# Attention and expert layer on one core: batch 1's queries projected ahead of the first denominators, the first quotient in two halves, and two edits of the queues

## The chip, the core and the metric

The kernel runs on one core of a Trainium2 chip. The core has five engines that work side by side, each through its own instructions in order: TensorE (matrix products, PE in the profile, with its weight loads as PEld), VectorE (DVE), ScalarE (ACT), GpSimd (POOL) and SyncE (SP, which here only starts transfers). Sixteen DMA engines move data between the main memory, the on-chip memory and back. TensorE writes into PSUM, a small memory of eight banks; VectorE and ScalarE read it from there. The metric is the time on the device in microseconds (us), the median of several runs.

## The reference

Four batches, four heads, 1088 tokens, head size 32; the second part has 4352 = 4 x 1088 tokens of 128 numbers, 8 experts, and a hidden size of 1024. All is in single precision.

```
phi(x) = (S1 x) outer (S2 x), 8 x 8 = 64 features          # S1, S2: 8 x 32
kv = sum over tokens of phi(k) v ; z = sum of phi(k)
x  = phi(q) kv / (phi(q) z + 1e-6), heads side by side      # 4352 x 128
P  = exp(x w_gate - max), then 8 times: rows to sum 1, columns to sum N/E
out = sum over experts e of P[:, e] * (relu(x w1[e]) w2[e])
```

## The kernel before

**Expert layer.** Most of the work is `x w1[e]`, relu, `w2[e]`. The 4352 tokens are cut into groups; `items` are pairs of a group and an expert, and `blocks` cut each item by the hidden size. A group is of two token tiles (functions `two`, and `eight` or `seven`, which saves products by a Strassen-like scheme) or of three (`four`, `twenty`, with more sums and fewer products). `step(c)` of a block is one product with `w1` (`first`, L914) and a relu on ScalarE into `hb` or `hx` (L918); the second products (`into`, L1099) follow eight steps later and add up in four PSUM banks. VectorE makes sums and differences of hidden tiles (`less`, `do`). GpSimd makes sums and differences of `w2`: `sums_of_two` and `sums_of_four`. The latter (tile `ws`, 1 MB) are made once per expert (L242), stored to memory (L246), and loaded again for each later group (L230). GpSimd also multiplies a group's tokens by the routing weights (`prepare_x`, `weigh`, tile `xe`, L678), which SyncE loads by `pT` (`weights_of`, L674). Some (group, expert) pairs are worked off before the routing weights are known; their results are `kept` unweighted, weighted later by `weigh_kept` and added.

**Attention.** Batch 0 takes a way of its own so that the first tokens are ready early. Its queries are cut into three chunks: columns 0 to 511, 512 to 799, 800 to 1087. For a chunk c, `query_products(c)` (L376) makes both factors of the features, `multiply(c, i)` (L384, VectorE) multiplies them, `fractions(c, 1)` and `fractions(c, 0)` (L392) make denominators and numerators, and `divide(c)` (L403 to L410) makes the quotient on VectorE: the denominators are turned by blocks of 32, one column in 32 is kept, made reciprocal, spread and turned back, and multiplied into `xT`. `keys_kept(0)` (L362, ScalarE) copies the sums of batch 0's keys, `kvz`, which `fractions` need. Batches 1 to 3 go through `queries_ab(b)` (L426 and the copy L429 into `qab`), which projects the queries, transfers that repeat the factors (`qa`, `qb`, `repeat_a`, `repeat_b`), and `attention(b)`. `transpose_q(b)` (L297, VectorE) turns a batch's queries.

**Order.** Where `tc.manual_schedule` names engines, their instructions go in the order of the program; elsewhere a planner orders them, and `tc.keep_in_program_order` fixes single ones. The first stretch names VectorE, TensorE and ScalarE, the second VectorE and TensorE. `fill(n)` puts as many expert steps into the attention's order as pay for n: after the first quotient `fill(1.25)` gives two steps of the first block, then come `fractions(1, 1)` and `fractions(1, 0)`, then two more steps. The first group is columns 0 to 511 in two tiles of 256. Its four steps go through token tile t fastest:

```
f, t = 2 * q + c // 2, c % 2
first(k, f, t * n, (t + 1) * n, h[c], k % 2)
```

The four PSUM banks called `a` go round: every `bank()` takes the next.

Of the kernel before, what the change touches and what calls it, by code (L numbers as in the profile page):

```python
# [10 lines left out]
F32 = mybir.dt.float32  # L11
U32 = mybir.dt.uint32
Act = mybir.ActivationFunctionType
Alu = mybir.AluOpType
# [36 lines left out]
def kernel(  # L51
# [12 lines left out]
    nc = tc.nc  # L64
    P = nc.NUM_PARTITIONS
# [146 lines left out]
    stored, stored_four = {}, {}  # L212
# [13 lines left out]
    def sums_of_four(e, w2):  # L226

        ws = pools[0].tile([P, len(FORMS), FO // 4, H2], F32, tag="ws4", name="ws4")
        if e in stored_four:
            nc.sync.dma_start(out=ws, in_=stored_four[e])  # L230
            return ws

        def blocks(bs):
            b = w2[:, bs[0][1]::4, H2 * bs[0][0]:H2 * (bs[0][0] + 1)].unsqueeze(1)
            if len(bs) == 1:
                return b
            step = (bs[1][1] - bs[0][1]) * DM + (bs[1][0] - bs[0][0]) * H2
            return AP(tensor=b.tensor, offset=b.offset, ap=[b.ap[0], [step, 2], *b.ap[2:]])

        c = 0  # L240
        for ns, x, y, off in FOURS:
            tc.keep_in_program_order(nc.gpsimd.tensor_tensor(ws[:, c:c + len(ns)], blocks(x), blocks(y),  # L242
                                                             op=Alu.subtract if off else Alu.add))
            c += len(ns)
        stored_four[e] = dram.tile([P, len(FORMS), FO // 4, H2], F32, name=f"ws4{e}")
        nc.sync.dma_start(out=stored_four[e], in_=ws)  # L246
        return ws


# [45 lines left out]
    def transpose_q(b, lo=0, hi=S):  # L295
        to = kT if b == 1 else qT
        nc.vector.transpose(out=to[:, lo:hi], in_=loaded["q", b].rearrange("p a d -> p (a d)")[:, lo:hi])  # L297
# [94 lines left out]
            nc.tensor.matmul(t[64 * i:64 * (i + 1), 0:n], kvz[:, m, i].rearrange("p h d -> p (h d)"),  # L392
                             phs[0][:, i, lo:hi], start=True, stop=True, tile_position=(0, 64 * i))

    def divide(c):


        lo, hi = chunks[c]
        n = hi - lo
        nb = n // 32  # L400
        pn, pd = (queries.pop((0, c, "pn", m)) for m in range(2))
        rd = wk.tile([P, 512], F32, tag="rd", name="rd")
        nc.vector.transpose(out=rd[:, 0:n], in_=pd[:, 0:n])  # L403
        rc = wk.tile([P, 16], F32, tag="rc", name="rc")[:, 0:nb]
        nc.vector.tensor_scalar_add(rc, rd[:, 0:n].rearrange("p (b r) -> p b r", r=32)[:, :, 0], 1e-6)
        nc.vector.reciprocal(rc, rc)
        rd = wk.tile([P, 512], F32, tag="rd", name="rd")
        nc.vector.transpose(out=rd[:, 0:n].rearrange("p (b r) -> p b r", r=32),
                            in_=rc.unsqueeze(2).to_broadcast([P, nb, 32]))
        nc.vector.tensor_tensor(xT[:, lo:hi], pn[:, 0:n], rd[:, 0:n], op=Alu.mult)  # L410

# [494 lines left out]
    def first(k, f, lo, hi, out, flip):  # L908

        j = blocks[k][0]  # L910
        ph = bank()[:, 0:hi - lo]
        for s in (1, 0) if flip else (0, 1):
            sl = slice(H2 * s, H2 * (s + 1))
            nc.tensor.matmul(ph[sl], loaded_w[j][0][:, P * f + H2 * s:P * f + H2 * (s + 1)],  # L914
                             sources[j][:, lo:hi], start=True, stop=True, tile_position=(0, H2 * s))
        if len(out.shape) == 3:
            ph = ph.rearrange("p (t n) -> p t n", t=2)
        nc.scalar.activation(out=out, in_=ph, func=Act.Relu)  # L918

    def two(k):  # L920

        j, q = blocks[k]
        n = groups[items[j][0]][1]
        h, ts, (later_h, earlier_h, t13) = hs[k] = room_of(k)

        def step(c):
            f, t = 2 * q + c // 2, c % 2
            first(k, f, t * n, (t + 1) * n, h[c], k % 2)

        def less(out, a, b):  # L930
            nc.vector.tensor_tensor(out, a, b, op=Alu.subtract)  # L931

        def sums(c):
            if direct_of(j):
                return

            if k == len(blocks) - 1:
                if c == 4:
                    less(ts[0], h[1], h[0])
                    less(ts[2], h[3], ts[0])  # L940
                    less(ts[1], h[3], h[1])
                    less(ts[3], h[2], ts[2])
            elif c == 4:
                less(t13, later_h, earlier_h)
            elif c == 5:
                less(ts[2], h[3], ts[0])
                less(ts[3], h[2], ts[2])

        return 4, step, sums
# [159 lines left out]
    def steps():  # L1109

        todo, sums_at, t = {}, {}, 0
        for k in range(len(blocks) + 5):
            if k == len(blocks) - 2:
                ctx.enter_context(tc.manual_schedule(engines={engines.DVE, engines.PE, engines.Activation}))
            if k == len(blocks):
                for i, ps in enumerate(last_products()):
                    todo.setdefault(t + i, []).extend(ps)
            if k < len(blocks):
                j, q = blocks[k]
                g, e = items[j]  # L1120
                lo, n, tiles, es, weighted = groups[g]
                if q == 0:
                    for i in (j, j + 1, j + 2 if 0 < j and j + 2 < first_weighted else j):
                        if i < len(items) and i not in sources and (pools or i < first_weighted):
                            prepare_x(i)
                        if i < len(items) and i not in loaded_w and (pools or i < first_weighted):
                            prepare_w(i)
                if j == 0 and q == 2:
                    prepare_w(2)
                if q == 1 and j + 1 < first_weighted and not direct_of(j + 1) and loaded_w[j + 1][2] is None:  # L1130
                    w1, w2, _ = loaded_w[j + 1]
                    w = w1, w2, sums_of_two(items[j + 1][1], w2)
                    loaded_w.update({i: w for i in loaded_w if items[i][1] == items[j + 1][1]})
                if q == 0:
                    if weighted and 1 <= es.index(e) <= es[0] + 1:
                        weigh_kept(g, es.index(e) - 1)
                if k == len(blocks) - HELD:
                    kept_to_sums(g)
                m, step, sums_ = (four if tiles == 3 else two)(k)
                products = twenty if tiles == 3 else eight if g in DIRECT else seven  # L1140
            for c in range(m if k < len(blocks) else 4):
                if k < len(blocks):
                    step(c)
                for do in sums_at.pop(t, ()):
                    do()
                while soon:
                    soon.pop(0)()
                for b, p in todo.pop(t, ()):
                    second(b, p)
                if k < len(blocks) and c == 0:  # L1150
                    for i in range(2, 10):
                        sums_at.setdefault(t + i, []).append(lambda i=i, f=sums_: f(i))
                    if k < len(blocks) - 2:
                        for i, ps in enumerate(products(k)):
                            todo.setdefault(t + LAG + i, []).extend((k, p) for p in ps)
                share = n / 480 * (16 / 15 if g in DIRECT else 1)
                if k >= len(blocks):
                    while later:
                        later.pop(0)()
                elif later and (tiles == 3 or c % 2 or share > 0.9):  # L1160
                    later.pop(0)()
                yield share
                t += 1
        while soon:
            soon.pop(0)()
        while later:
            later.pop(0)()
# [11 lines left out]
    with tc.manual_schedule(engines={engines.DVE, engines.PE, engines.Activation}):  # L1179
        st = projections()  # L1180
        repeated(st)
        halves = ((0, NT // 2), (NT // 2, NT))
        transpose_k(0, halves)
        keys_ab(0, halves)
        transpose_q(0, *chunks[0])
        query_products(0)
        for part_ in range(3):
            keys_products(0, part_)
        keys_sums(0)
        for i in range(2):  # L1190
            multiply(0, i)
        keys_kept(0)
        transpose_q(1)
        transpose_q(0, chunks[0][1])
        fractions(0, 1)
        queries_ab(1)
        fractions(0, 0)
        query_products(1)
        repeat_a(1)
        repeat_b(1)  # L1200
        divide(0)
        load_q(2)
    with tc.manual_schedule(engines={engines.DVE, engines.PE}):
        for i in range(2):
# [66 lines left out]
```

## Time and profile before

| | before |
|---|---|
| time, median of 3 | 920.12 us (920.08 to 920.75) |
| span of the profile | 918.0 us |
| PE busy | 911.2 us (99%) |
| DVE busy | 678.9 us (74%) |
| ACT busy | 421.6 us (46%) |
| POOL busy | 204.0 us (22%) |
| DMA, mean | 140 GB/s |

The span runs from the first to the last instruction of the profiled execution; busy times are those of each engine within it. In the lines, `L392` is the line of the kernel, `a<-ph,kvz` says which tile is written from which, and `<-` in the waits says what the engine waited for. A matrix product in single precision leaves two records for each half of the array, so four for one `first`. Matrix products overlap one another, and the ends of their records are modelled.

### The profile page before, as it was taken

What the parts mean: (1) busy time and instruction counts of PE and PEld (TensorE: products, weight loads), DVE (VectorE), ACT (ScalarE), POOL (GpSimd) and SP (SyncE); (2) the same over time, 40 slices, a digit from 0 to 9 for tenths busy, and PEclk for the clock granted to TensorE, in tenths of its full rate; (3) what the DMA queues carried; (4) which work ended last, traced back from release to release, by engine and by line L of the source; (5) the groups of instructions that cost most, each with busy time, mean ns of one, the idle gap of its engine ahead of it and who ended that gap; (6) DMA issues with size and microseconds to landing.
All of it is one profiled execution on the core that took longest, in us unless ns stands there. A gap on an engine that the chain in (4) does not pass through costs nothing.

```text
span 918.0 us, 18893 instructions
## 1 busy us (share of the span) xinstructions
PE 911.2 (99%) x7442; PEld 637.4 (69%) x7442; DVE 678.9 (74%) x1173; ACT 421.6 (46%) x915; POOL 204.0 (22%) x212
## 2 busy tenths in 40 slices
PE   9999999999999999999999999999999999999997
PEld 6777544466666677777777777777777655556886
DVE  7678699888776798666975656956567976758665
ACT  3455555554444454444544444544445444445443
POOL 3121100175545421201210010110100243210220
PEclk9999999999999999999999999999999999999999
DMA  9994100213454535534364343454445456453640
GB/s 254 308 273 163 54 1 1 70 64 127 148 150 139 186 119 174 165 110 150 114 185 134 117 143 112 132 187 127 133 122 165 130 170 195 162 166 92 177 153 13
DMA packets 91305, 128.15 MB, mean 140 GB/s; under 512 B 25392, under 2 KB 69504, under 8 KB 86480
## 3 DMA queue, kind: packets, MB, share of 16 engines
q1 hardware_dynamic: 88384, 121.42, 42.7%
q0 software_dynamic: 1600, 5.36, 2.1%
q8 instruction: 58, 0.95, 0.4%
q10 hardware_dynamic: 1232, 0.16, 0.1%
q14 instruction: 31, 0.25, 0.1%
HBM read 107.88 MB, written 19.05 MB: 138 GB/s over the span
## 4 chain that ended last, share of the span: by engine, by line
PE 97%; DVE 2%; ACT 1%; issue 0%; POOL 0%; DVEq 0%; POOLq 0%
PE a L914 51%; PE s L1099 41%; PE a L347 1%; PE a L462 1%; PE a L114 1%; DVE hb L931 1%; PE a L314 0%; PE s L376 0%; PE a L426 0%; PE s L392 0%; DVE cs L602 0%; PE a L496 0%; PE a L392 0%; ACT hb L918 0%; DVE rs L596 0%
## 5 line engine op out<-in xcount | busy, mean ns | idle before, releaser
L914 PE MATMUL a<-xe,w 128*64 128x256 f32 (+1 forms) x2560 | 569.8, 470 | 0.0
L918 ACT ACTIVATE hb<-a 128x256 f32<-128x256 f32 (+4 forms) x408 | 195.0, 480 | 241.5 <-PE a L914 209.3
L914 PEld LDWEIGHTS a<-xe,w 128*64 128x64 f32 x2560 | 263.0, 137 | 50.8 <-issue 1.8
L918 ACT ACTIVATE hx<-a 128x256 f32<-128x256 f32 (+1 forms) x360 | 167.3, 465 | 213.5 <-PE a L914 191.6
L1099 PE MATMUL s<-hb,ws 128*64 128x256 f32 (+3 forms) x1312 | 256.1, 395 | 0.2 <-DVE hb L931 0.2
L1099 PE MATMUL s<-hx,ws 128*64 128x256 f32 x1280 | 233.9, 379 | 0.0
L978 DVE TENSOR_TENSOR hb<-hb 128x512 f32<-128x512 f32 (+1 forms) x204 | 133.5, 664 | 102.8 <-ACT hb L918 98.8
L978 DVE TENSOR_TENSOR hx<-hx 128x512 f32<-128x512 f32 (+1 forms) x204 | 149.8, 744 | 65.0 <-ACT hx L918 60.2
L1099 PEld LDWEIGHTS s<-hb,ws 128*64 128x64 f32 x1312 | 134.9, 137 | 87.8 <-issue 64.5
L678 POOL TENSOR_TENSOR xe<-xT,xe 128x768 f32<-128x768 f32 (+2 forms) x41 | 80.3, 1958 | 481.2 <-DMA xe<-pT 377.0
L1099 PEld LDWEIGHTS s<-hx,ws 128*64 128x64 f32 x1280 | 132.7, 137 | 71.6 <-issue 50.3
L914 PE MATMUL a<-xT,w 128*64 128x416 f32 (+3 forms) x512 | 119.7, 462 | 0.0
L1099 PE MATMUL s<-hb,w 128*64 128x256 f32 (+3 forms) x536 | 114.2, 408 | 0.0
L1099 PE MATMUL s<-hx,w 128*64 128x256 f32 x384 | 76.0, 379 | 0.0
L931 DVE TENSOR_TENSOR hb<-hb 128x416 f32<-128x416 f32 (+7 forms) x84 | 60.7, 723 | 18.0 <-ACT hb L918 14.0
L1099 PEld LDWEIGHTS s<-hb,w 128*64 128x64 f32 x536 | 54.1, 137 | 19.0 <-issue 6.5
L914 PEld LDWEIGHTS a<-xT,w 128*64 128x64 f32 x512 | 48.9, 137 | 25.5 <-issue 15.7
L242 POOL TENSOR_TENSOR ws<-w 128x256 f32<-128x256 f32 (+1 forms) x70 | 60.5, 899 | 8.1 <-DMA w<-in_moe_w_dram 5.2
L931 DVE TENSOR_TENSOR hx<-hx 128x256 f32<-128x256 f32 (+1 forms) x65 | 39.5, 612 | 24.0 <-ACT hx L918 22.8
L1099 PEld LDWEIGHTS s<-hx,w 128*64 128x64 f32 x384 | 40.8, 137 | 6.6
L978 DVE TENSOR_TENSOR pqg<-hb 128x512 f32<-128x512 f32 x68 | 40.5, 637 | 0.0
L978 DVE TENSOR_TENSOR pqg<-hx 128x512 f32<-128x512 f32 x68 | 35.0, 554 | 0.0
(181 smaller groups left out, 485.0 us busy)
## 6 DMA issues: line engine op xcount, KB each, us to landing
w<-in_moe_w_dram SPq DMA_DIRECT2D x82, 512.0 KB, 5.5
ws<-ws SPq DMA_DIRECT2D x34, 1024.0 KB, 5.0
xe<-pT SPq DMA_DIRECT2D x34, 384.0 KB, 4.1
ws<-ws SPq DMA_DIRECT2D x12, 512.0 KB, 3.6
ph<-qa SPq DMA_DIRECT2D x12, 288.0 KB, 4.7
rb<-qb SPq DMA_DIRECT2D x3, 1152.0 KB, 7.2
pb<-pT SPq DMA_DIRECT2D x6, 384.0 KB, 8.3
kx<-in_k_dram SPq DMA_DIRECT2D x4, 544.0 KB, 4.0
```

Of the source, the lines that this page charges most:

```text
L114: nc.tensor.matmul(warm[:, 0:P], ones, ones, start=True, stop=True)
L242: tc.keep_in_program_order(nc.gpsimd.tensor_tensor(ws[:, c:c + len(ns)], blocks(x), blocks(y), op=Alu.subtract if off else Alu.add))
L347: nc.tensor.matmul(pv[64 * s:64 * (s + 1), i], kp[0:n, H * t + h].rearrange("p i j -> p (i j)"), vx[0:n, slots[h], t, :], start=(t == 0 an ...
L462: nc.tensor.matmul(pn[64 * s:64 * (s + 1), t, 2 * i:2 * i + 2].rearrange("p h d -> p (h d)"), ph[:, i, s, 64 * t:64 * (t + 1)], kvs[b % 2] ...
L678: tc.keep_in_program_order(nc.gpsimd.tensor_tensor(out, x, pb, op=Alu.mult))
L914: nc.tensor.matmul(ph[sl], loaded_w[j][0][:, P * f + H2 * s:P * f + H2 * (s + 1)], sources[j][:, lo:hi], start=True, stop=True, tile_posit ...
L918: nc.scalar.activation(out=out, in_=ph, func=Act.Relu)
L931: nc.vector.tensor_tensor(out, a, b, op=Alu.subtract)
L978: nc.vector.tensor_tensor(out if not isinstance(out, tuple) else places(*out), places(*a), places(*b) if isinstance(b, tuple) else b, op=A ...
L1099: nc.tensor.matmul(sums[g][i][H2 * s:H2 * (s + 1), n * place:n * (place + 1)], w, x, start=c == 1, stop=c == per, tile_position=(0, H2 * s))
```

## The change

It has four parts. First, the queries of batch 1 are turned (`transpose_q(1)`) ahead of the products of chunk 0, and projected (`queries_ab(1)`) ahead of the first denominators, so that TensorE has work while ScalarE copies `kvz`. Second, `divide` can work in parts, and the first quotient is done in two halves of 256 columns; the first block's steps go through the hidden tile fastest, so that the first two need the first half alone. Third, the sums of `sums_of_four` are stored by GpSimd's queue instead of SyncE's, so that SyncE's later loads don't stand behind a store that waits for GpSimd. Fourth, `weigh_kept` comes in the second block of an item instead of the first.

```diff
         stored_four[e] = dram.tile([P, len(FORMS), FO // 4, H2], F32, name=f"ws4{e}")
-        nc.sync.dma_start(out=stored_four[e], in_=ws)
+        tc.keep_in_program_order(nc.gpsimd.dma_start(out=stored_four[e], in_=ws))
         return ws
...
-    def divide(c):
+    def divide(c, parts=1):
         lo, hi = chunks[c]
-        n = hi - lo
+        n = (hi - lo) // parts
         nb = n // 32
         pn, pd = (queries.pop((0, c, "pn", m)) for m in range(2))
...
+        for i in range(0, hi - lo, n):
+            rd = wk.tile([P, 512], F32, tag="rd", name="rd")
+            nc.vector.transpose(out=rd[:, 0:n], in_=pd[:, i:i + n])
+            rc = wk.tile([P, 16], F32, tag="rc", name="rc")[:, 0:nb]
+            nc.vector.tensor_scalar_add(rc, rd[:, 0:n].rearrange("p (b r) -> p b r", r=32)[:, :, 0], 1e-6)
+            nc.vector.reciprocal(rc, rc)
+            rd = wk.tile([P, 512], F32, tag="rd", name="rd")
+            nc.vector.transpose(out=rd[:, 0:n].rearrange("p (b r) -> p b r", r=32),
+                                in_=rc.unsqueeze(2).to_broadcast([P, nb, 32]))
+            nc.vector.tensor_tensor(xT[:, lo + i:lo + i + n], pn[:, i:i + n], rd[:, 0:n], op=Alu.mult)
...
         def step(c):
-            f, t = 2 * q + c // 2, c % 2
-            first(k, f, t * n, (t + 1) * n, h[c], k % 2)
+            f, t = (c % 2, c // 2) if k == 0 else (c // 2, c % 2)
+            first(k, 2 * q + f, t * n, (t + 1) * n, h[2 * f + t], k % 2)
...
-                if q == 0:
-                    if weighted and 1 <= es.index(e) <= es[0] + 1:
-                        weigh_kept(g, es.index(e) - 1)
+                if q == 1 and weighted and 1 <= es.index(e) <= es[0] + 1:
+                    weigh_kept(g, es.index(e) - 1)
...
         keys_sums(0)
+        transpose_q(1)
         for i in range(2):
             multiply(0, i)
         keys_kept(0)
-        transpose_q(1)
         transpose_q(0, chunks[0][1])
+        queries_ab(1)
         fractions(0, 1)
-        queries_ab(1)
         fractions(0, 0)
         query_products(1)
         repeat_a(1)
         repeat_b(1)
-        divide(0)
+        divide(0, 2)
         load_q(2)
```

More of the change, by code (lines that the diff above doesn't have):

```diff
@@ L393, in fractions @@
                              phs[0][:, i, lo:hi], start=True, stop=True, tile_position=(0, 64 * i))
-    def divide(c):
+    def divide(c, parts=1):
         lo, hi = chunks[c]
-        n = hi - lo
+        n = (hi - lo) // parts
         nb = n // 32
         pn, pd = (queries.pop((0, c, "pn", m)) for m in range(2))
[L402 to L410, printed above, removed]
+        for i in range(0, hi - lo, n):
[8 more added lines that the diff above has]
+            nc.vector.tensor_tensor(xT[:, lo + i:lo + i + n], pn[:, i:i + n], rd[:, 0:n], op=Alu.mult)
     def queries_ab(b):
```

## The prediction

> **What bounds the kernel now.** I read first the page's slices and the chain of work that ended last, which say that TensorE is never out of work for long:
>
> ```profile
> PE   9999999999999999999999999999999999999997
> PEclk9999999999999999999999999999999999999999
> ...
> PE 97%; DVE 2%; ACT 1%; issue 0%; POOL 0%; DVEq 0%; POOLq 0%
> ```
>
> Then the busy time by stretches, to see where the remaining 3% lie. The columns are length, then busy time of PE, PEld, DVE, ACT and POOL:
>
> ```profile
> 12.60:13.40 0.80, 0.17 (x7) 0.03 (x4) 0.80 (x2) 0.52 (x2) 0.00 (x0) 1.00 1.21 304
> 13.40:18.45 5.05, 5.05 (x36) 2.51 (x36) 4.11 (x10) 1.74 (x5) 2.25 (x4) 1.00 1.12 278
> 18.45:100.00 81.55, 81.55 (x1076) 61.71 (x1076) 63.31 (x111) 38.74 (x102) 15.79 (x27) 1.00 0.76 229
> 200.00:912.00 712.00, 712.00 (x5548) 514.73 (x5545) 513.82 (x880) 318.04 (x678) 166.80 (x133) 1.00 0.45 141
> ```
>
> From 13.4 us on TensorE has no hole: 81.55 of 81.55 us, and 712.00 of 712.00. A busy PE need not be PE at its peak, so I also read the starts of single matmuls. A pair on the two halves of the array starts every 0.216 us at 256 columns, 0.430 at 512, and outside the changes of shape (0.05 to 0.16 us each) I find no late start between 200 us and the end. The only place with free time is the stretch from 12.6 to 13.4 us. The waits of TensorE in the whole run name it:
>
> ```profile
> PE a L114 <- POOL own L116: 1.0, 1, 1.0
> PE a L392 <- ACT kvz L362: 0.6, 1, 0.6
> PE s L1099 <- DVE hb L931: 0.2, 1, 0.2
> ```
>
> The chain of waits from 12 us shows what follows it, and VectorE's timeline shows how close that engine runs beside it (start, duration):
>
> ```profile
> 13.39 1.08 PE a L392 x4
> 14.47 0.98 PE a L426 x12
> 15.45 0.86 PE a L392 x4
> 16.31 1.17 PE s L376 x8
> 17.48 1.01 PE a L914 x8
> 18.49 1.15 PE s L392 x8
> ```
>
> ```profile
> 14.55 0.72 DVE L403 STREAM_TRANSPOSE rd<-a 128x512 f32<-128x512 f32 x1 [0.46 <-PE a L392]
> 15.30 0.17 DVE L405 TENSOR_SCALAR rc<-rd 128x16 f32<-128x16 f32 x1
> 15.51 0.25 DVE L406 RECIPROCAL rc<-rc 128x16 f32<-128x16 f32 x1
> 15.79 0.71 DVE L408 STREAM_TRANSPOSE rd<-rc 128x512 f32<-128x512 f32 x1
> 16.61 0.69 DVE L410 TENSOR_TENSOR xT<-a,rd 128x512 f32<-128x512 f32 x1
> 17.58 0.82 DVE L384 TENSOR_TENSOR ph<-ph,s 128x288 f32<-128x288 f32 x2 [0.28 <-PE s L376]
> ```
>
> The reader is to see that the quotient (14.55 to 17.30) and the second chunk's products (17.58 to 18.40) end just as TensorE wants them: L914 starts at 17.41, L392 at 18.45. Two engines run level here, so work added to VectorE is not hidden.
>
> [...] a transposition takes 0.72 us at 512 columns and 0.44 at 288, the mean of L384's products falls only from 0.67 to 0.45. [...] Here the seven stores of ws4 take 0.33 us each on SyncE's queue, and what they cost there is the wait ahead of them (111.4 us in 7, longest 17.0, for GpSimd's sums). [...] the hole of 0.8 us did not lower the clock (1.00), and I take the same for a wait of 1.6.
>
> **The change, part by part.**
>
> *Batch 1's queries earlier.* On VectorE the turn of the queries (L297, 12.14 to 13.36 by start of the next) goes ahead of the two products L384 (10.94 to 12.14). Their sum is the same: turn 10.94 to 12.16, products to 13.36. The queries' load has landed by 10.67 by its semaphore, so 0.27 us are left. On TensorE the last L347 leaves the array free at 12.60. The projections (L426, 0.98) now stand next; their kT is there at 12.2, so they fill the hole: 12.70 (0.10 for the change of shape, as L347 to L914 at 30.5) to 13.68. The denominators L392 then start at 13.68 instead of 13.39; kvz is there at 13.35, the products at 13.4. The numerators follow at 14.59 (0.91 as before), L376 at 15.55 (0.96), and TensorE is free for L914 at 16.72 (1.17) instead of 17.41. So TensorE has 0.69 us in hand, but the denominators are 0.29 us later. The copy qab and the DMAs behind it (qa, qb) start about 1.6 us earlier; nothing on TensorE waits for them, and the wait for rb that follows (4.6 us on VectorE at 32.8) holds no matmul.
>
> *First quotient in two halves, first steps reordered.* Before, VectorE's first read came 1.16 us after the denominators' start (14.55 less 13.39): now 13.68 + 1.16 = 14.84. The whole chain took 17.30 - 14.55 = 2.75. For 256 columns I take the rows at 512 and 288: transposition 0.72 - 256 x (0.28/224) = 0.40, twice; product 0.69 - 256 x (0.23/224) = 0.43; the two small operations and the gaps as before. That is 2.75 - 0.32 - 0.31 - 0.26 = 1.86, checked by the 288-column chain at 19.60 to 21.58 (1.98). The first half is ready at 16.70. L914 starts 0.10 after it (as before: 17.30 to 17.41), 16.80, with TensorE free since 16.72. Its two steps need only columns 0 to 255, since the new order takes both F tiles on token tile 0 first. They end at 17.75.
>
> Next on TensorE are the fractions of chunk 1 (L392), which wait for the products L384 of chunk 1. These stand in VectorE's order behind the second half, which is the wait that the change adds: second half 16.64 to 18.50 (an independent operation starts 0.06 before the last ends), products 18.44 to 19.26, L392 at 19.31. Before, it was 18.45. Behind the waiting L392 stand all later matmuls; TensorE sits idle from 17.75 to 19.31, 1.56 us, where it lost 0.13 before. Net: 19.31 - 18.45 = 0.86 us later. The extra VectorE work is 2 x 1.86 - 2.75 = 0.97; the chain also starts 0.29 later and loses the 0.28 us wait that stood before L384. 0.97 + 0.29 - 0.28, less 0.06 at each of two joints, is again 0.86.
>
> The bounds: with a transposition of 0.38 or 0.48 and a product of 0.40 or 0.46, a half is 1.79 to 2.05, so the delay is 0.7 to 1.2 us. Afterwards TensorE is at work without a hole to 912 us, so no later slack can take the delay back; transposition of the keys (L302) and the second quotient move with it, and L314 finds its kT at 20.6, before TensorE comes (21.2).
>
> *Stores by GpSimd's queue.* It removes SyncE's seven waits. It adds seven issues on GpSimd; the trace has the like of them (xd, L486: 0.59 us; xt's 576 KB), so 0.6 x 7 = 4 us beside 204 us busy of 918. Behind each stand the kept sums and the next weighted tokens xe. The tightest case before: xe was ready at 240.17 (238.17 + 2.00), and TensorE's first weight load with it was at 241.05. It was that late since its load stood behind the store (227.76) and the kept product before it waited 8.53 us for pb. Both loads may now go earlier by up to 14 us, so 0.6 us more on GpSimd doesn't show. Worth: 0, since TensorE waited for neither.
>
> *Kept sums one block later.* The order on GpSimd stays xe, sums, kept. At the end the sums are done at 877.7 and TensorE loads them at 882.4. A block there is 3.88 us, so at worst 0.8 us are left. Worth: 0.
>
> Sum: +0.86 us, so 920.12 + 0.86 = 921.0.
>
> **Rivals.** (a) Faster: if the second half hid behind TensorE's work, as the change means it to, L392 would start at 17.85 (17.75 + 0.10) and the end come 0.60 earlier: 919.5. For it speaks that TensorE is free 0.69 us earlier; against it VectorE's order, in which nothing stands between half two and the products. At most the hole and the late start go, 0.80 + 0.13: 919.2. (b) Slower by more: the queries land 0.5 us or more later (DMA is at 1.10 of its share there, and only 0.27 us are in hand), and turn, products and denominators move: up to 0.8 us more, 921.8. (c) A new hole later: a store on GpSimd holds up xe or ws4; if the 0.6 us of each of seven came through, 4 us more, 925. Against it stands the freed SyncE queue. (d) The delay is lost in the changes of shape near 22 to 23 us (0.16 and 0.21 us): 920.6, which is no change.
>
> **How the numbers follow.** Forecast 0.60, (a) 0.15, (b) 0.10, (c) 0.05, (d) 0.10. The bound of 0.2% is 1.84 us. The forecast, (a) and (d) lie within it. Faster by 1.84 us would need more than the 0.93 us of free time that the trace has: 0.03. Slower by 1.84 needs (c), or (b) with the upper bound of the halves (1.2 + 0.8 = 2.0): 0.08. Same 0.89. The range goes from 919.2 (a) to 922.1 (b with the upper bound).
>
> **What would show it.** Right: TensorE waits at L392 for DVE ph L384 for about 1.5 us from 17.8 to 19.3; no wait for ACT kvz; L426 starts near 12.7; L914 near 16.8; the quotient's rows come twice, 256 columns each, about 0.40 us a transposition; 200 to 912 without a hole. Wrong: L392 of chunk 1 before 18.4, a wait of the turn for DMA qx, or a wait of TensorE for GpSimd past 180 us.

## The result, and the profile after

| | before | after |
|---|---|---|
| time, median of 6 | 920.13 us (919.5 to 920.75) | 923.0 us (922.62 to 923.8) |
| ratio, 95% interval | | 1.0031 [1.0018, 1.0044] |
| span of the profile | 918.0 us | 921.1 us |

The change made the kernel 0.3% slower, and the time lies above the range that was forecast (919.2 to 922.1). First the waits of TensorE after the change (total, times, longest):

```profile
PE s L1101 <- DVE hx L980: 2.5, 2, 2.3
PE a L114 <- POOL own L116: 1.0, 1, 1.0
PE s L392 <- DVE ph L384: 0.7, 1, 0.7
PE a L314 <- DVE kT L302: 0.4, 1, 0.4
PE s L1101 <- DVE hb L933: 0.2, 1, 0.2
```

The wait for `kvz` is gone, the wait of L392 for the products is there and is smaller than forecast, and the first line is new. TensorE's timeline shows where that one stands (start, duration, and in brackets how long TensorE was idle ahead and for what):

```profile
198.69 0.59 PE L915 MATMUL a<-xe,w 128*64 128x256 f32 x2
201.56 0.65 PE L1101 MATMUL s<-hx,ws 128*64 128x256 f32 x4 [2.28 <-DVE hx L980]
...
205.48 0.65 PE L1101 MATMUL s<-hx,ws 128*64 128x256 f32 x4 [0.23 <-DVE hx L980]
```

From the starts of single matmuls, TensorE has nothing to do for about 2.4 us before 201.56 and for about 0.4 before 205.48. Up to there the chain of waits runs 0.30 us late (L314 at 20.81 instead of 20.51, L915 at 189.81 instead of 189.52). 0.3 + 2.4 + 0.4 = 3.1 us, the whole difference of the spans (921.1 - 918.0). So at most a tenth of the loss is in the part that I had worked out, and nine tenths are in a place where I saw none.

The chain that ended last names VectorE for it, one operation of 7.73 us. The two timelines of VectorE at that point, before and then after:

```profile
192.62 0.56 DVE L741 TENSOR_TENSOR z<-x,z 128x384 f32<-128x384 f32 x1 [1.77 <-ACT x L750]
193.12 0.69 DVE L978 TENSOR_TENSOR hx<-hx 128x512 f32<-128x512 f32 x1
```

```profile
192.91 7.73 DVE L742 TENSOR_TENSOR z<-x,z 128x384 f32<-128x384 f32 x1 [1.91 <-ACT x L751]
200.57 0.94 DVE L980 TENSOR_TENSOR hx<-hx 128x512 f32<-128x512 f32 x1
```

The same sum of 384 columns takes 0.56 us before and 7.73 after. It is not a sum for TensorE at all (it gathers a group's unweighted results), but the sum of `hx` that TensorE needs stands behind it and starts at 200.57 instead of about 193.1. What GpSimd does meanwhile, before and then after:

```profile
182.97 8.62 POOL L242 TENSOR_TENSOR ws<-w 128x256 f32<-128x256 f32 x10
197.62 1.92 POOL L678 TENSOR_TENSOR xe<-xT,xe 128x768 f32<-128x768 f32 x1 [6.03 <-DMA xe<-pT]
199.50 8.85 POOL L242 TENSOR_TENSOR ws<-w 128x256 f32<-128x256 f32 x10
```

```profile
192.45 0.60 POOL L246 DMA_DIRECT2D ws<-ws  x1 [0.30 <-POOL ws L242]
193.07 1.83 POOL L679 TENSOR_TENSOR xe<-xT,xe 128x768 f32<-128x768 f32 x1
194.85 6.10 POOL L242 TENSOR_TENSOR ws<-w 128x256 f32<-128x256 f32 x10
201.25 0.61 POOL L246 DMA_DIRECT2D ws<-ws  x1 [0.30 <-POOL ws L242]
```

Before, GpSimd rests for 6.03 us ahead of `xe`, because SyncE issued the load of `xe` behind the store. SyncE's issues, before and then after:

```profile
191.61 0.32 SPq L246 DMA_DIRECT2D ws<-ws  x1
191.98 0.43 SPq L674 DMA_DIRECT2D xe<-pT  x1
```

```profile
175.63 0.81 SPq L675 DMA_DIRECT2D xe<-pT  x2
```

After, that load is the second of these two and went out at 176.0, 16 us earlier, so GpSimd issues the store and runs straight on for 7.9 us (193.07 to 200.95). VectorE's sum begins during the issue and ends only 0.3 us before that run does. Both engines read from the main on-chip memory, SBUF; the sum of `z` reads both of its operands there.

### The profile page after: what moved, and what is told of

Read it like the earlier page. It is cut to its first block, busy times and chain, and to the rows that moved or that the text cites. A ratio compares the mean times of both kernels' runs of the same rounds, so it can differ in the third digit from the quotient of the medians.

```text
span 921.1 us, 18903 instructions
## 1 busy us (share of the span) xinstructions
PE 911.3 (99%) x7442; PEld 533.7 (58%) x7442; DVE 682.1 (74%) x1178; ACT 421.9 (46%) x915; POOL 207.6 (23%) x219
## 3 DMA queue, kind: packets, MB, share of 16 engines
q0 software_dynamic: 2608, 12.70, 3.8%
## 4 chain that ended last, share of the span: by engine, by line
PE 94%; DVE 4%; ACT 1%; DMA 1%; issue 0%; SPq 0%; DVEq 0%; ACTq 0%
PE a L915 49%; PE s L1101 42%; PE a L347 1%; DVE z L742 1%; PE a L463 1%; DVE hb L933 1%; DMA kx<-in_k_dram 1%; PE a L314 0%; PE a L427 0%; DVE hx L980 0%; PE s L376 0%; PE s L392 0%; DVE cs L603 0%; PE a L497 0%; DVE w L742 0%
## 5 line engine op out<-in xcount | busy, mean ns | idle before, releaser
L915 PE MATMUL a<-xe,w 128*64 128x256 f32 (+1 forms) x2560 | 516.2, 470 | 0.0
L915 PEld LDWEIGHTS a<-xe,w 128*64 128x64 f32 x2560 | 200.1, 137 | 86.6 <-issue 1.6
L1101 PE MATMUL s<-hb,ws 128*64 128x256 f32 (+3 forms) x1312 | 228.7, 395 | 0.2 <-DVE hb L933 0.2
L1101 PE MATMUL s<-hx,ws 128*64 128x256 f32 x1280 | 205.4, 379 | 2.5 <-DVE hx L980 2.5
L1101 PEld LDWEIGHTS s<-hb,ws 128*64 128x64 f32 x1312 | 104.9, 137 | 116.8 <-issue 86.9
L1101 PEld LDWEIGHTS s<-hx,ws 128*64 128x64 f32 x1280 | 102.4, 137 | 103.5 <-issue 74.2
L915 PE MATMUL a<-xT,w 128*64 128x416 f32 (+3 forms) x512 | 119.7, 462 | 0.0
L1101 PE MATMUL s<-hb,w 128*64 128x256 f32 (+3 forms) x536 | 106.9, 408 | 0.0
L1101 PE MATMUL s<-hx,w 128*64 128x256 f32 x384 | 67.8, 379 | 0.0
L915 PEld LDWEIGHTS a<-xT,w 128*64 128x64 f32 x512 | 49.0, 137 | 25.5 <-issue 15.7
L1101 PEld LDWEIGHTS s<-hb,w 128*64 128x64 f32 x536 | 46.8, 137 | 24.0 <-issue 6.5
L1101 PEld LDWEIGHTS s<-hx,w 128*64 128x64 f32 x384 | 33.2, 137 | 11.5
```

The costliest lines, as they stand in the source:

```text
L1101: nc.tensor.matmul(sums[g][i][H2 * s:H2 * (s + 1), n * place:n * (place + 1)], w, x, start=c == 1, stop=c == per, tile_position=(0, H2 * s))
```

## The experiments

Two questions stood at first: which part of the change makes the loss, and, if it is the stores, what about them: the transfer issued by GpSimd itself, the run without a pause that the earlier load allows, or the two together.

**Which part of the change.** Four kernels: three with some parts alone, one with the stores left out. Parts 1 and 2 were not tried apart.

```diff
# stores alone, on the kernel before
-        nc.sync.dma_start(out=stored_four[e], in_=ws)
+        tc.keep_in_program_order(nc.gpsimd.dma_start(out=stored_four[e], in_=ws))
```

> Kernel before with the stores of ws4 on GpSimd's queue alone; the order on TensorE, VectorE and ScalarE stays that of before. Theory 1 (the stores' queue makes the late hole: the next weighted tokens come earlier, GpSimd works without a pause from about 183 to 201 us, and a VectorE operation with two on-chip inputs starves beside it): z<-x,z near 192.6 takes several us instead of 0.56, TensorE waits about 2 to 3 us near 201 us, time +2 to +3 us, 922 to 923. Theory 2 (the front's shift of 0.3 us is needed for the collision, or the kept sums are): z<-x,z stays below 2.2 us, no wait of TensorE near 201, time within 0.5 of before.

```diff
# parts 1 and 2 alone: the changed kernel with these undone
-        tc.keep_in_program_order(nc.gpsimd.dma_start(out=stored_four[e], in_=ws))
+        nc.sync.dma_start(out=stored_four[e], in_=ws)
-                if q == 1 and weighted and 1 <= es.index(e) <= es[0] + 1:
-                    weigh_kept(g, es.index(e) - 1)
+                if q == 0:
+                    if weighted and 1 <= es.index(e) <= es[0] + 1:
+                        weigh_kept(g, es.index(e) - 1)
```

> Kernel before with the first two parts alone: queries of batch 1 earlier, first quotient in halves with the reordered steps; stores and kept sums as before. Theory 1: the front costs 0.3 us (L392 of chunk 1 at 18.75 instead of 18.45) and nothing comes back later, no hole near 201: 920.4. Theory 2 (the front's shift alone makes the late collision): a hole of 2 to 3 us near 201, 923.

Part 4 alone is the last edit of that diff, turned round, on the kernel before:

> Kernel before with the kept sums one block later, nothing else. Theory 1: no part in it, no hole of TensorE beyond those of before, within 0.3 us of before. Theory 2 (the kept sums' place makes GpSimd's pile): a hole above 1 us.

The changed kernel with the first edit of that diff only, so all but the stores:

> The changed kernel with the stores of ws4 back on SyncE's queue. Theory 1: the hole near 201 us goes, z<-x,z takes about 0.6 us, the front's 0.3 stays: 920.4, 2.6 below the changed kernel. Theory 2: the hole stays, 923.

| kernel | time | ratio to before | sum of `z` |
|---|---|---|---|
| stores alone | 923.78 us | 1.0038 [1.0025, 1.0050] | 7.70 us |
| parts 1 and 2 alone | 919.96 | 0.9994 [0.9985, 1.0002] | 0.56 |
| kept sums later alone | 920.16 | 1.0003 [0.9994, 1.0011] | 0.56 |
| all but the stores | 919.83 | 0.9997 [0.9989, 1.0006] | 0.56 |

The stores alone make the whole loss; the other parts, alone or together, can't be told from no change. The 0.3 us that was expected of the front in two of them (920.4) doesn't show in the times, and the stores alone came out a little above the expected 922 to 923. The trace of the stores alone has the same picture, VectorE and GpSimd:

```profile
193.70 7.70 DVE L741 TENSOR_TENSOR z<-x,z 128x384 f32<-128x384 f32 x1 [1.93 <-ACT x L750]
```

```profile
193.21 0.60 POOL L246 DMA_DIRECT2D ws<-ws  x1 [0.30 <-POOL ws L242]
193.82 1.82 POOL L678 TENSOR_TENSOR xe<-xT,xe 128x768 f32<-128x768 f32 x1
195.60 6.10 POOL L242 TENSOR_TENSOR ws<-w 128x256 f32<-128x256 f32 x10
```

TensorE's new holes in it are 2.36 us at 202.31 and six of 0.19 to 0.42 in the 4.4 us behind it, 4.04 together. The other 1.1 us of its longer span (923.1 less 918.0) come from a wait at 35.12, long before the first of these stores. The profile puts it down to ScalarE's `hb`, but that was done at 34.19. The matmul (L462) also reads `ph`, and VectorE's product for it (L453) starts at 34.06 instead of 32.79, since the transfer `rb` lands later in this execution. Neither the kernel before nor the change has this wait in its trace, and three of the kernels below have one of 0.2 to 0.6 us there, with and without a loss in their times, so I count it as no part of the stores' cost.

**The earlier load without the transfer by GpSimd.** The stores stay on SyncE's queue, but behind the next load of `xe`, on the kernel before. GpSimd then runs without a pause, and issues nothing.

```diff
-        nc.sync.dma_start(out=stored_four[e], in_=ws)
+        pending.append((stored_four[e], ws))
...
         xe = weights_of(e, lo, t * n, "xe")
+        while pending:
+            to, ws = pending.pop()
+            tc.keep_in_program_order(nc.sync.dma_start(out=to, in_=ws))
```

> Kernel before, stores of ws4 still on SyncE's queue but each issued behind the next weighted tokens' load, so that GpSimd's run of xe and sums follows the first sums without a pause and without a transfer issued by GpSimd. Theory P (a run of GpSimd's operations without a pause is enough to starve a VectorE operation with two on-chip inputs): z<-x,z near 192.6 takes 6 to 8 us and TensorE waits 2 to 3 us near 201, 922.5 to 923. Theory D (the VectorE operation must begin while GpSimd issues a transfer): z takes at most 2.3 us, as long as the xe beside it, no wait above 0.5 us near 201, within 0.5 of before.

Measured: 919.72 us, ratio 0.9994 [0.9985, 1.0002]. GpSimd, then VectorE:

```profile
187.71 4.53 POOL L242 TENSOR_TENSOR ws<-w 128x256 f32<-128x256 f32 x6
192.20 1.82 POOL L678 TENSOR_TENSOR xe<-xT,xe 128x768 f32<-128x768 f32 x1
193.98 10.92 POOL L242 TENSOR_TENSOR ws<-w 128x256 f32<-128x256 f32 x10
```

```profile
193.27 1.17 DVE L744 TENSOR_TENSOR z<-x,z 128x384 f32<-128x384 f32 x1 [1.76 <-ACT x L753]
194.36 1.21 DVE L981 TENSOR_TENSOR hx<-hx 128x512 f32<-128x512 f32 x1
```

The run without a pause is there, but the sum of `z` waits only for the end of `xe` (193.27 + 1.17 = 194.44, `xe` ends at 194.02), and then the two engines take turns: ten sums of GpSimd need 10.92 us instead of 6.10, and VectorE's operations about 1.2 instead of 0.7. No hole of TensorE follows. The run alone is not the cause.

**The transfer by GpSimd without the earlier load.** The store on GpSimd's queue, and on SyncE's queue a copy of one small block of `ws` (32 KB) in its old place, so that `xe` comes as late as before.

```diff
-        nc.sync.dma_start(out=stored_four[e], in_=ws)
+        tc.keep_in_program_order(nc.gpsimd.dma_start(out=stored_four[e], in_=ws))
+        gate = dram.tile([P, H2], F32, name=f"gate{e}")
+        nc.sync.dma_start(out=gate, in_=ws[:, len(FORMS) - 1, FO // 4 - 1])
```

> Kernel before with the stores of ws4 on GpSimd's queue, and on SyncE's queue a small copy of the last sums (32 KB) that waits for GpSimd as the store did, so that the next weighted tokens come as late as before. Theories P and D both: GpSimd pauses after the store, z<-x,z stays below 1.3 us, no wait near 201, within 0.5 us of before. Theory Q (the transfer itself, in GpSimd's queue, does the harm): z long and a hole of 2 to 3 us as in the changed kernel.

Measured: 920.15 us, ratio 1.0001 [0.9992, 1.0009]. GpSimd, then VectorE:

```profile
192.79 0.60 POOL L246 DMA_DIRECT2D ws<-ws  x1 [0.30 <-POOL ws L242]
197.60 2.12 POOL L680 TENSOR_TENSOR xe<-xT,xe 128x768 f32<-128x768 f32 x1 [4.21 <-DMA xe<-pT]
```

```profile
193.53 0.56 DVE L743 TENSOR_TENSOR z<-x,z 128x384 f32<-128x384 f32 x1 [1.76 <-ACT x L752]
```

The same transfer, issued by the same engine at the same place, cost nothing here, where GpSimd rests 4.21 us behind it. Neither half makes the loss; both together do.

**Is it the operand?** The kernel with the stores alone, where the sum of `z` reads its first operand from PSUM:

```diff
-            add_now(z, p, z)
+            add_now(z, s if g == PLAIN - 1 else p, z)
```

> Stores on GpSimd's queue as in the store-only kernel, and the one VectorE sum z<-x,z of the last unweighted group reads its first input from PSUM instead of the copy of it. Theory of the shared input (P or D): this sum takes about 0.5 us beside GpSimd's run; the next operation with two on-chip inputs may be caught in its place. If it is not, no hole; if it is, it stands out with 5 to 7 us. Theory O (VectorE is held as a whole, whatever it reads): z itself takes about 7.7 us again.

Measured: 922.03 us, ratio 1.0019 [1.0012, 1.0026]. VectorE:

```profile
193.96 0.56 DVE L741 TENSOR_TENSOR z<-s,z 128x384 f32<-128x384 f32 x1 [1.91 <-ACT x L750]
194.46 7.36 DVE L978 TENSOR_TENSOR hx<-hx 128x512 f32<-128x512 f32 x1
201.74 0.94 DVE L978 TENSOR_TENSOR pqg<-hx 128x512 f32<-128x512 f32 x1
```

The sum of `z` begins during GpSimd's issue (193.49 to 194.09) as it did with the stores alone, and takes 0.56 us; the next operation, with both operands in SBUF, is caught in its place. It began at 194.46, when the issue was over and `xe` was running. So the operation with both operands in SBUF was held (7.36 us), the one with an operand in PSUM was not (0.56), and the held one needn't have begun during the issue. Half of the loss stays.

**Alone, first try.** A small kernel that computes none of the reference: VectorE adds 384 columns again and again beside runs of ten GpSimd sums of 256 columns, without a transfer, with one issued by GpSimd ahead of the run, and with that and one operand in PSUM.

> Not the reference's computation at all: VectorE alone with sums of 384 columns, 24 in a row, beside GpSimd with ten sums of 256 columns in a row, six times each in three stretches: without a transfer, with a 1 MB store issued by GpSimd ahead of the ten, and with that store while VectorE's first input lies in PSUM. Undisturbed a sum takes about 0.56 us. Theory P: single sums of 6 to 7 us in the first two stretches. Theory D: 1 to 1.5 us at most in the first, 6 to 8 us in the second only. Both: no sum above 0.7 us in the third.

It didn't show the effect. With two operands in SBUF the engines took turns in both phases, one for one (ten sums of GpSimd 9.71 us behind a transfer); no VectorE operation was above 1.35 us, and the means were alike (738 ns with the transfer, 726 without); with one in PSUM it was 557 ns. But all the sums of GpSimd wrote the same tile, so each waited for the one before on GpSimd's own semaphore (13.0 us of idle time ahead of 180 sums), which the kernel's sums don't. The next experiment takes these waits out.

**Alone, without those pauses.** Each sum has a tile of its own. The transfer is also smaller here, 32 KB instead of 1 MB, and waits for a result of GpSimd as the kernel's store does. One execution, with each phase three times.

```diff
-                for i in range(10):
-                    tc.keep_in_program_order(nc.gpsimd.tensor_tensor(y[:, 0:256], w[:, 1024:1280], w[:, 1280:1536], op=Alu.add))
+                y = big.tile([P, 10, 256], F32, name=f"y{name}{r}")
+                for i in range(10):
+                    if name == "pause" and i == 4:
+                        sums(y[:, i], y[:, i - 1], e)
+                    else:
+                        sums(y[:, i], b, e)
```

> Not the reference's computation: VectorE adds two 384-column operands in SBUF (in the last phase one of them in PSUM) beside runs of ten GpSimd sums of 256 columns that each have a tile of their own, so that no sum waits for another. Theory: it is the issue of a transfer by GpSimd, with no pause behind it, [...]. Then without it (plain) VectorE's operations take about 0.96 us each beside the sums, as in the phases with pauses; behind GpSimd's transfer (gdma) the first one takes 6 to 8 us; with one sum made to wait for the one before it (pause) it takes about 3 to 4 us, to the fifth sum; with the transfer issued by SyncE (sdma) 0.96 us again; from PSUM 0.56 us. Rival: the small experiment lacks something else that the kernel has (broadcast operands, what the other engines do), and no phase shows an operation above 2.5 us.

One pass of each phase from GpSimd's timeline, without the last phase; `yplain` has no transfer, `ysdma` one by SyncE, `ygdma` one by GpSimd, `ypause` too, with a fifth sum that reads the fourth's result:

```profile
24.84 10.02 POOL L41 TENSOR_TENSOR yplain<-w 128x256 f32<-128x256 f32 x10
...
80.51 0.56 POOL L57 DMA_DIRECT2D storegdma<-xgdma  x1 [0.30 <-POOL xgdma L41]
81.09 6.83 POOL L41 TENSOR_TENSOR ygdma<-w 128x256 f32<-128x256 f32 x10
...
143.44 2.75 POOL L41 TENSOR_TENSOR ypause<-w 128x256 f32<-128x256 f32 x4
146.27 0.93 POOL L41 TENSOR_TENSOR ypause<-ypause,w 128x256 f32<-128x256 f32 x1
147.16 5.02 POOL L41 TENSOR_TENSOR ypause<-w 128x256 f32<-128x256 f32 x5
...
200.16 10.02 POOL L41 TENSOR_TENSOR ysdma<-w 128x256 f32<-128x256 f32 x10
```

VectorE in the `gdma` pass shown:

```profile
80.68 7.66 DVE L65 TENSOR_TENSOR dgdma<-w 128x384 f32<-128x384 f32 x1
```

A sum of GpSimd takes 1.00 us where the engines take turns (10.02 / 10) and 0.68 where VectorE stands still (6.83 / 10) or reads one operand from PSUM (6.86 / 10; VectorE's operations 0.56). Behind its own transfer GpSimd runs on undisturbed to the last sum: VectorE's longest operations there were 7.66 and 7.65 us in two of three passes. With the one pause they were 3.57, 3.58 and 3.58, to the end of the fourth sum, and from then on the engines took turns (5.02 for five). With SyncE's transfer or none, none was above 1.0. This is the kernel's effect with nothing of the kernel left, and a transfer of 32 KB is enough for it. The first pass of the `gdma` phase wasn't caught: VectorE's operation, begun during the issue, took 1.07 us, and the ten sums 10.08. It is the first transfer that GpSimd issues in this program, and its issue took 0.69 us instead of 0.56; why it left VectorE alone, the runs don't say.

**The whole change, with the cause taken away in two ways.** First by the deferred store on SyncE's queue, as above but on the changed kernel:

> The whole change, but with the stores left on SyncE's queue, behind the next load of the weighted tokens instead of ahead of it. Theory: the loads come as early as with the change, SyncE waits for nobody, and GpSimd issues no transfer, so the sum of z takes 0.6 to 1.5 us, there is no hole of TensorE at 201 us, and the time is 919.3 to 920.3. Rival (the earlier load, or the pause-free run with the other two parts in place, is enough to make the hole): 922 to 923.5.

Then with the store left to GpSimd, and a pause behind it:

```diff
         tc.keep_in_program_order(nc.gpsimd.dma_start(out=stored_four[e], in_=ws))
+        for i in range(2):
+            tc.keep_in_program_order(nc.gpsimd.tensor_tensor(rest[i + 1], rest[i], rest[i], op=Alu.add))
```

> The whole change, its stores on GpSimd's queue included, with two GpSimd additions of 16 columns behind each store, the second reading the first's result, so that GpSimd pauses once for its own semaphore right behind the issue. Theory (the issue followed by a run without a pause starves VectorE): the sum of z starts in that pause and takes 0.6 to 1.5 us, the operations behind it alternate with GpSimd's, there is no hole of TensorE at 201 us, and the time is 919.5 to 920.5, with the weighted tokens loaded as early as with the change. Rival ([...] the pause comes too early to release it): the sum of z still takes 6 to 8 us and the time stays at 922 to 923.5.

The first: 919.92 us, ratio 0.9998 [0.9989, 1.0006], the sum of `z` 1.28 us, no hole at 201 us. The second: 919.8 us, ratio 0.9991 [0.9983, 0.9999]. Its GpSimd, then VectorE:

```profile
192.69 0.60 POOL L248 DMA_DIRECT2D ws<-ws  x1 [0.30 <-POOL ws L244]
193.31 1.12 POOL L250 TENSOR_TENSOR rest<-rest 128x16 f32<-128x16 f32 x2
194.39 2.26 POOL L683 TENSOR_TENSOR xe<-xT,xe 128x768 f32<-128x768 f32 x1
196.61 10.39 POOL L244 TENSOR_TENSOR ws<-w 128x256 f32<-128x256 f32 x10
```

```profile
193.17 0.56 DVE L746 TENSOR_TENSOR z<-x,z 128x384 f32<-128x384 f32 x1 [1.92 <-ACT x L755]
193.67 0.69 DVE L984 TENSOR_TENSOR hx<-hx 128x512 f32<-128x512 f32 x1
```

Everything of the change is in it, the transfer by GpSimd, the early load and the run behind it; two additions of 16 columns give the 3 us back. They also put `xe` 1.3 us later, so that the sum of `z` is through before it; that the hold is over is seen behind it, where the ten sums take 10.39 us in turns with VectorE, instead of 6.10. Its interval ends just below 1, but those of other versions overlap it, so it isn't shown to be faster than the kernel before.

## Why the prediction was wrong

**The step that failed** is "Stores by GpSimd's queue": "Worth: 0, since TensorE waited for neither". Its parts about the transfers held. An issue on GpSimd costs 0.60 us (forecast 0.6). SyncE's wait for GpSimd's sums (111.4 us before) is gone, and the load of `xe` went out 16 us earlier (forecast up to 14). Neither `xe` nor `ws` kept TensorE waiting, and the wait of TensorE for GpSimd past 180 us, which I had named as a sign against me, isn't in the list: it names VectorE. What I left out, and so put at nothing, is the third party. I asked who waits for GpSimd's results, and not what GpSimd's run does to VectorE, which reads the same memory. The earlier load takes away the 6.03 us of rest ahead of `xe`, and behind the issue VectorE's two-operand sum doesn't get in until that run is nearly over: 7.73 us instead of 0.56, and 2.4 + 0.4 us of TensorE.

The trace of before has a smaller case that I could have weighed: a VectorE sum of 384 columns with both operands in SBUF takes 2.18 us there, not 0.56, beside `xe` (197.62 to 199.54):

```profile
197.78 2.18 DVE L738 TENSOR_TENSOR z<-z,w 128x384 f32<-128x384 f32 x1
```

With the deferred store, too, VectorE waited for one instruction and then the two took turns (1.17 us, then 1.21). Behind a transfer by GpSimd it waited for nearly all of eleven instructions in the kernel (7.73 us), for all ten in the small one (7.66 in the pass shown). So the trace of before alone would have led me to one instruction's wait, by my estimate (the 2.18 above, `xe` takes 1.83 us) some 2 us of VectorE, and not to 7.7.

**Rival (c)**, "a new hole later", 925 us at 0.05, comes nearest in kind and size (3.1 of 4 us), but that is luck. Its reason was another: nothing held up `xe` or `ws4`, `xe` came earlier, and one place of seven makes the loss, not 0.6 us at each.

**Queries earlier**: right. L427 starts at 12.79 (forecast 12.70), the denominators at 13.82 (13.68), L915 at 16.97 (16.80); the hole of 0.80 us is gone. A wait of the turn for `qx` showed up, which I had put down as a sign against me: 0.42 us. It ends at 11.32, and the turn is over in time: L427 starts with no idle time ahead of it, so the wait costs nothing.

**Halves**: the wait that I forecast is there, but a term was much too large. VectorE after the change:

```profile
14.97 0.45 DVE L404 STREAM_TRANSPOSE rd<-a 128x256 f32<-128x256 f32 x1 [0.48 <-PE a L392]
...
17.47 0.20 DVE L407 RECIPROCAL rc<-rc 128x8 f32<-128x8 f32 x1
17.59 0.41 DVE L384 TENSOR_TENSOR ph<-ph,s 128x288 f32<-128x288 f32 x1
17.92 0.44 DVE L409 STREAM_TRANSPOSE rd<-rc 128x256 f32<-128x256 f32 x1
18.28 0.42 DVE L384 TENSOR_TENSOR ph<-ph,s 128x288 f32<-128x288 f32 x1
18.62 0.41 DVE L411 TENSOR_TENSOR xT<-a,rd 128x256 f32<-128x256 f32 x1
```

A half takes 1.90 us (14.97 to 16.87; forecast 1.86). But the products L384 don't stand behind the second half, as I had them: they run between its operations. In the source they do come behind it: `divide(0, 2)` ends the first stretch with a fixed order and `multiply(1, i)` begins the second. In the trace the order isn't kept across that seam; what let the products pass is not shown. So L392 of chunk 1 starts at 18.75, not at 19.31, and TensorE's wait in front of it is 0.89 us counted as in the forecast, not 1.56 (the list says 0.7, by the modelled ends). The granted clock was 1.00 over that wait (17.75 to 18.75), and over the hole of 2.4 us too (198 to 206).

The forecast was 0.86 us later and this trace shows 0.30, but about 0.1 of that stands ahead of the whole change: the last L347 starts at 12.64 instead of 12.54, and from 12.04 to 12.98 over all eleven traces of the whole computation. Counted from that start, L392 of chunk 1 comes 5.90 or 5.91 us later in the six kernels with the old front and 6.05 to 6.12 in the five with the new one. So the front costs 0.14 to 0.22 us, about a quarter of the forecast at most: less of VectorE's added work stood in TensorE's way than I had it. In the time this can't be seen either way (0.9994 [0.9985, 1.0002]).

**Kept sums**: right, 0 (1.0003 [0.9994, 1.0011]). The stores alone lose as much without it, so it has no part in the loss that the intervals could show.

**Open**: why VectorE stays out of a GpSimd run that follows an issue by GpSimd, what in the pause lets it in, and why one pass of the small kernel wasn't caught. The runs show when it happens.

## What to carry to other kernels

When a transfer moves to GpSimd's queue, look at what GpSimd runs directly behind the issue, and at which VectorE operations with two SBUF operands fall into that run; ask it even where nobody waits for GpSimd's results. If there are some in front of TensorE's work, leave the issue to SyncE, or put a short pair of operations behind it, the second reading the first's result; both took the loss away here (919.92 and 919.8 us instead of 923.0). An operand read from PSUM spared the one operation that read it here (0.56 us), and the next one was caught (7.36). And a wait that is removed (here SyncE's, and with it 6.03 us of GpSimd's rest) may have been what gave a third engine its turn.

## What the hardware showed that was not expected

- A VectorE sum with both operands in SBUF waited for nearly all of a GpSimd run that followed a transfer issued by GpSimd, where GpSimd didn't have to wait within that run: 7.73, 7.70 and 7.36 us in three kernels, 7.66 and 7.65 in two of three passes of the small one, but 1.07 in the other.
- One wait of GpSimd for its own semaphore ended it (3.58 us, to the fourth of ten sums). With one right behind the issue it didn't come up (0.56 us).
- Without such a transfer, or with SyncE's, the two engines took turns, in the small kernel one instruction each; there ten GpSimd sums of 256 columns took 10.02 us instead of 6.83, and VectorE's sums of 384 columns 0.96 us instead of 0.56.
- With a shorter run behind the issue the wait was shorter. In the change's trace a sum of `hb` at 229.71 took 4.22 us: it fell behind the third of the seven stores, which only two GpSimd operations (3.62 us) follow. It cost TensorE nothing; behind the second store GpSimd rested for 9.17 us, and no operation of VectorE within that rest took over 0.69 us.
